# Loading and turning the first group's inputs in another way: attention with pooled keys into a mixture of four feed-forward branches

## The chip, the cores and the metric

The kernel runs on one core of one Trainium2 chip. The metric is the device time of one execution in microseconds; lower is better. Five engines work side by side, each on its own list of instructions: PE (matrix products, with weight loads shown as PEld), DVE (vector), ACT (scalar functions and copies), POOL and SP. Transfers between HBM and the on-chip memory are issued here by SP and by POOL and run on 16 DMA engines.

## The reference

```python
# attention: q, k, v are (8 batches, 8 heads, 576 tokens, 64)
k_p = k.reshape(B, H, 72, 8, D).mean(axis=3)      # 576 keys pooled to 72
v_p = v.reshape(B, H, 72, 8, D).mean(axis=3)
attn = softmax(q @ k_p.T / sqrt(64))              # over the 72 pooled keys
x = (attn @ v_p) -> rows (batch, token), columns (head, dim): 4608 x 512
# mixture: four branches, weighted by domain_probs
p = domain_probs / (domain_probs.sum(-1) + 1e-9)  # 4608 x 4
out = sum over e of p[:, e] * (relu(x @ w1[e]) @ w2[e])   # w1: 512 x 1024, w2: 1024 x 512
```

All inputs and the output are F32 in HBM; the products are done in bf16 with F32 sums.

## The kernel before

The 4608 tokens are cut into 36 tiles of 128, four tiles to a group of 512 tokens, nine groups. A step is one group with one branch, so there are 36 steps; each has 12 slots in which `up` (L457, eight blocks of `relu(x @ w1)`, ACT at L461) for the next step alternates with `down` (L490) and `collect` (L501, L505) of this step. Work of later tiles is put into slots by a hand-written plan (`at`, `plan_tile`, `plan_batch`). The order of every engine is the order in which the kernel writes its instructions; nothing reorders them.

Before the steps stands a head, also written out by hand, that gets group 0 through attention and through branch 0. For each tile t of group 0:

- the queries are cast to bf16 by ACT (`split_q`, L570) and turned by four PE products (`turn_q`, L310) and an ACT copy to `qT` (L314);
- `scores` (L320, one PSUM buffer `sc`), the maximum `maxima` (L334), the subtraction `less` (L338) on DVE, the exponential `expo` on ACT (L351 for tiles 0 and 1, L358 for 2 and 3);
- tiles 0 and 1: `attn_T` turns the unnormalised weights (L394, copy L395), `sums_by_products` gets the sums on PE (L640, L645, L647), `context_rows` multiplies by the values (L410) and divides (L419, `x_sb` in two halves), `turn_x` turns the result (L654) and ACT copies it into `xT` (L657);
- tiles 2 and 3: `normalise` divides on DVE first (L372 to L380), then `attn_T` and `context` (L440, copy to `xT` L446);
- `up_tile` (L473, relu L477) does the up-projection of one tile in two halves of four blocks, `down(0, t)` the second product, `collect(0, t)` the weighting.

The keys of batch 0 are folded from 8 to 1 on DVE in three parts of rows (`fold_keys0`, L589 and L593), turned on PE (`turn_keys0`, L600) and copied to `kT` by DVE (`take_keys0`, L613). The values are pooled by eight products with an identity (`sum_values0`, L619) and spread into a block form `vbd` by DVE (`spread_values0`, L628). `idle_products` (L576) are products with zeros that fill PE's waits.

The transfers of the head: SP loads all of group 0's queries in one transfer `qg` (L130), token `4p + c` on partition p, in pieces of 1 KB; then the domain weights of group 0 in the same token order (`dp0`, L134) and those of the other 32 tiles (`dpr`, L139). POOL loads, with conversion to bf16, the first keys (L80, L84: two parts and a tail), the first values, then builds the identity and the small mask `own`, then loads `w1[0]`, `w2[0]`, `w1[1]` and so on (L116, L122); from the ninth on each POOL load waits for the one eight before it.

The domain weights of group 0 are normalised by four small DVE operations in the head (`domain_probs0`, L205 to L208). Those of the other groups are normalised in slot 8 of step 0 on 32 partitions (`domain_probs`, L215 to L220), turned by four F32 products (L226) and copied (L227). Since group 0's tokens are permuted over its four tiles, `collect` writes its output rows with a stride of four rows.

Of the kernel before, what the change touches and what calls it, by code (L numbers as in the profile page):

```python
# [10 lines left out]
ALU = mybir.AluOpType  # L11
AX = mybir.AxisListType
BF16 = mybir.dt.bfloat16
F32 = mybir.dt.float32
# [3 lines left out]
def kernel(  # L18
# [70 lines left out]
    def load_v(b):  # L89
        load_rows(vraw[b % 2], v[b])  # L90
# [30 lines left out]
    def load_w2(e):  # L121
        nc.gpsimd.dma_start(  # L122
            out=w2_sb[e][:], in_=moe_w2[e].rearrange("(fb p) d -> p fb d", p=P)
        )

    qg = raw.tile([P, H, TPG, D], F32, name="qg")
    nc.sync.dma_start(  # L130
        out=qg[:], in_=q[0][:, 0:G, :].rearrange("h (p c) d -> p h c d", c=TPG)
    )
    dp0 = const.tile([P, TPG, E], F32, name="dp0")
    nc.sync.dma_start(  # L134
        out=dp0[:], in_=moe_domain_probs[0:G].rearrange("(p c) e -> p c e", c=TPG)
    )
    NL = NT - TPG
    dpr = const.tile([NL, P, E], F32, name="dpr")
    nc.sync.dma_start(  # L139
        out=dpr[:], in_=moe_domain_probs[G:NTOK].rearrange("(t p) e -> t p e", p=P)  # L140
    )

    still = const.tile([P, G], BF16, name="still")
    nc.vector.memset(still[:], 0.0)  # L144
    load_rows(kraw[0], k[0], ((0, 2), (2, 4)))
    load_v(0)
    ident = const.tile([P, P], BF16, name="ident")
    make_identity(nc, ident[:])

# [2 lines left out]
    for sign, base in ((1, 0), (-1, SP - 1)):  # L152
        nc.gpsimd.affine_select(
            out=own[:], in_=own[:], compare_op=ALU.is_ge, fill=0.0,
            base=base, channel_multiplier=sign,
            pattern=[[sign * (P - PW), NPAIR], [sign * P, 2], [-sign * SP, 2]],
        )
    load_w1(0)
    load_w2(0)
    load_w1(1)  # L160
    for c in range(TPG):
        qrow[c] = qpool.tile([P, H, D], BF16, name="qrow")
    load_k(1)
    ident32 = const.tile([NL, NL], F32, name="ident32")
    make_identity(nc, ident32[:])
    load_w1(2)
    load_q(TPG)
    load_w2(1)
# [31 lines left out]

    p_sb = const.tile([P, E, NT], F32, name="p_sb")

    def domain_probs0():
        ds0 = const.tile([P, TPG], F32, name="ds0")
        nc.vector.reduce_sum(out=ds0[:], in_=dp0[:], axis=AX.X)  # L205
        nc.vector.tensor_scalar_add(out=ds0[:], in0=ds0[:], scalar1=1e-9)
        nc.vector.reciprocal(out=ds0[:], in_=ds0[:])
        nc.vector.tensor_tensor(  # L208
            out=p_sb[:, :, 0:TPG].rearrange("p e c -> p c e"), in0=dp0[:],
            in1=ds0[:].unsqueeze(2).to_broadcast([P, TPG, E]), op=ALU.mult,  # L210
        )

    def domain_probs():
        dsum = const.tile([NL, P], F32, name="dsum")
        nc.vector.reduce_sum(out=dsum[:], in_=dpr[:], axis=AX.X)  # L215
        nc.vector.tensor_scalar_add(out=dsum[:], in0=dsum[:], scalar1=1e-9)
        dinv = const.tile([NL, P], F32, name="dinv")
        nc.vector.reciprocal(out=dinv[:], in_=dsum[:])
        pn = const.tile([NL, E, P], F32, name="pn")
        nc.vector.tensor_tensor(  # L220
            out=pn[:], in0=dpr[:].rearrange("t p e -> t e p"),
            in1=dinv[:].unsqueeze(1).to_broadcast([NL, E, P]), op=ALU.mult,
        )
        pt = ps_t.tile([P, E, NL], F32, tag="t", name="pt")
        for e in range(E):
            nc.tensor.transpose(pt[:, e, :], pn[:, e, :], ident32[:])  # L226
        nc.scalar.copy(out=p_sb[:, :, TPG:NT], in_=pt[:])  # L227


    kT, vbd, pads = {}, {}, {}  # L230
# [264 lines left out]
    def collect(s, i):  # L495
        g, e = divmod(s, E)
        t = g * TPG + i
        ps = o_ps[t]
        if e == 0:
            accs[t] = accp.tile([P, DM], F32, name="acc")  # L500
            nc.vector.tensor_scalar_mul(  # L501
                out=accs[t][:], in0=ps[:], scalar1=p_sb[:, e, t:t + 1]
            )
        else:
            nc.vector.scalar_tensor_tensor(  # L505
                out=accs[t][:], in0=ps[:], scalar=p_sb[:, e, t:t + 1], in1=accs[t][:],
                op0=ALU.mult, op1=ALU.add,
            )
        if e == E - 1:
            rows = out[t * P:(t + 1) * P, :]  # L510
            if g == 0:
                rows = out[0:G, :].rearrange("(p c) d -> p c d", c=TPG)[:, i, :]
            nc.sync.dma_start(out=rows, in_=accs[t][:])


    SLOTS = 12
# [2 lines left out]
    def at(slot, fn, *args):  # L519
        plan.setdefault(slot, []).append((fn, args))  # L520
# [21 lines left out]
            if t + 3 < NT:  # L542
                at(slot + sum_v, load_q, t + 3)

    at(SLOTS - 4, domain_probs)
    at(SLOTS - 2, prep_k, 1)
    at(SLOTS, prep_kT, 1)
    at(SLOTS + 4, prep_v, 1)
# [18 lines left out]


    def split_q(c):
        nc.scalar.copy(out=qrow[c][:], in_=qg[:, :, c, :])  # L570
# [13 lines left out]

    def fold_keys0(p1, i0, i1):
        rows = kraw[0][0:p1, i0:i1]
        for n in (4, 2):
            w = n * D
            nc.vector.tensor_add(  # L589
                out=rows[:, :, 0:w], in0=rows[:, :, 0:w], in1=rows[:, :, w:2 * w]  # L590
            )
        twice = [p1, i1 - i0, 2, D]
# [22 lines left out]

    def sum_values0():
        ps = ps_h.tile([P, NB, D], F32, tag="h", name="v_ps")
        for r in range(POOL):
            nc.tensor.matmul(  # L619
                ps[:], lhsT=ident[:], rhs=vraw[0][:, :, r * D:(r + 1) * D],  # L620
                start=(r == 0), stop=(r == POOL - 1),
            )
        return ps

    def spread_values0(ps):
        vbd[0] = prep.tile([P, NPAIR, 2, 2, D], BF16, name="vbd")
        for z in range(2):
            nc.vector.tensor_tensor(  # L628
                out=vbd[0][:, :, z],
                in0=ps[:, z:z + NPAIR].unsqueeze(2).to_broadcast([P, NPAIR, 2, D]),  # L630
                in1=mask_v[:, :, z], op=ALU.mult,
            )
# [15 lines left out]

    def turn_x(t, halves):
        n = KC // 2  # L650
        for i, pool, tag in ((0, ps_t, "t"), (1, ps_h, "h")):
            ps = pool.tile([P, n, P], BF16, tag=tag, name="xT_ps")
# [9 lines left out]
    idle_products(14)  # L662
    make_mask_v()
    split_q(0)
    split_q(1)
    turn_q(0)
    turn_q(1)
    for part in ((P, 0, 2), (P, 2, 4), (TAIL, 4, 5)):
        fold_keys0(*part)
        turn_keys0(*part)  # L670
        idle_products(2)
    take_keys0()
    scores(0)
    split_q(2)
    turn_q(2)
    idle_products(2)
    less_max(0)
    split_q(3)
    expo(0)
    spread_values0(sum_values0())  # L680
    scores(1)
    attn_T(0)
    maxima(1)
# [4 lines left out]
    turn_q(3)  # L688
    idle_products(1)
    turn_x(0, x_sb)  # L690
    less(1)
    expo(1)
    up_tile(0, 0, (0,))
    attn_T(1, copy=nc.vector.tensor_copy)
    up_tile(0, 0, (TPG,))
    sums_by_products(1)
    x_sb = context_rows(1, 2)
    scores(2)
    idle_products(2)
    turn_x(1, x_sb)  # L700
    less_max(2)
    expo(2)
    domain_probs0()
    up_tile(0, 1)
    scores(3)
    down(0, 0)
    normalise(2)
    less_max(3)
    collect(0, 0)
# [62 lines left out]
```

## Time and profile before

| | |
|---|---|
| median of 3 runs | 550.66 us (550.55 to 550.84) |
| profiled execution | 551.05 us |
| its span, first to last instruction | 548.6 us |
| granted TensorE clock, mean | 0.999 |
| busy PE, DVE, ACT, POOL | 536.1, 264.4, 213.0, 71.2 us |
| keys of batch 0 complete (end of the wait) | 9.38 us |
| first values product | 13.06 us |
| first `scores` | 12.15 us |
| first `up_tile` product | 18.43 us |
| first `up` product of step 1 | 35.57 us |

Times within the execution count from the first instruction. A line of the timeline gives the start, the length, the engine, the source line, what is written from what, the shapes, how many, and in brackets how long the engine had been idle and what ended that. A line of the chain gives the start, the length and the work that held the end of the program at that time.

### The profile page before, as it was taken

Reading aid. Unit: us, or ns where it says so; the run is one execution under the profiler, and the core shown is the slowest. Engines: PE = TensorE matmul, PEld = TensorE weight load, DVE = VectorE, ACT = ScalarE, POOL = GpSimd, SP = SyncE. Lnnn points to the kernel's source line nnn. Section 1 sums busy time; section 2 is a strip of 40 time slices with the busy share of each in tenths; the row PEclk is TensorE's granted clock in tenths of the full one; section 3 lists DMA queues with packets and bytes.
Section 4 is the critical chain, followed back from the end, with each engine's and each line's share of the span. In section 5 each row is a group of like instructions: output and inputs, shape, how many; then the busy total and the mean of one; then the engine's idle time right before and its main releaser. Section 6 shows DMA issues by size and latency. Waiting matters only on the chain.

```text
span 548.6 us, 7264 instructions
## 1 busy us (share of the span) xinstructions
PE 536.1 (98%) x2870; PEld 260.3 (47%) x2926; DVE 264.4 (48%) x458; ACT 213.0 (39%) x356; POOL 71.2 (13%) x120
## 2 busy tenths in 40 slices
PE   6899999999999999999999999999999999999997
PEld 2664554444444444444444444444444444444443
DVE  4775847444744446444554444744474444422223
ACT  3564653333333333333333333333333333333330
POOL 7234001121111101011011100101010000000000
PEclk9999999999999999999999999999999999999999
DMA  9999926656545553377436552335333421111002
GB/s 194 207 202 198 200 24 129 85 78 87 115 71 76 82 115 79 49 80 117 85 54 84 76 115 32 54 41 118 41 54 41 99 51 32 22 39 38 1 0 78
DMA packets 110689, 45.84 MB, mean 84 GB/s; under 512 B 87584, under 2 KB 106016, under 8 KB 110656
## 3 DMA queue, kind: packets, MB, share of 16 engines
q0 software_dynamic: 51472, 22.03, 32.8%
q1 hardware_dynamic: 59184, 23.35, 17.7%
q8 instruction: 23, 0.38, 0.3%
q14 instruction: 10, 0.08, 0.0%
HBM read 45.16 MB, written 9.44 MB: 100 GB/s over the span
## 4 chain that ended last, share of the span: by engine, by line
PE 95%; DMA 1%; DVE 1%; issue 1%; ACT 1%; POOL 0%; DVEq 0%; POOLq 0%
PE o_ps L490 45%; PE h_ps L457 44%; PE x_ps L410 2%; PE sc L320 2%; PE h_ps L473 1%; DMA kraw<-in_k_dram 1%; PE x_ps L440 1%; PE at_ps L394 0%; PE qT_ps L310 0%; ACT attnT L395 0%; ACT xT L657 0%; POOL kraw L80 0%; DVE mx L334 0%; DVE d_sb L338 0%; DVE acc L505 0%
## 5 line engine op out<-in xcount | busy, mean ns | idle before, releaser
L461 ACT ACTIVATE h_sb<-h_ps 128x512 bf16<-128x512 f32 x280 | 167.2, 597 | 296.5 <-PE h_ps L457 292.3
L457 PE MATMUL h_ps<-xT,w 128*128 128x512 bf16 x1088 | 271.8, 379 | 1.5
L490 PE MATMUL o_ps<-w,h_sb 128*128 128x512 bf16 x1130 | 270.0, 379 | 1.3
L490 PEld LDWEIGHTS <-h_sb 128*128 128x128 bf16 x1152 | 112.3, 98 | 133.8
L505 DVE SCALAR_TENSOR_TENSOR acc<-o_ps,p_sb,acc 128x512 f32<-128x512 f32 x108 | 81.0, 750 | 180.4 <-PE o_ps L490 177.7
L457 PEld LDWEIGHTS <-w 128*128 128x128 bf16 x1120 | 105.9, 98 | 116.9
L501 DVE TENSOR_SCALAR acc<-o_ps,p_sb 128x512 f32<-128x512 f32 x36 | 27.0, 749 | 59.6 <-PE o_ps L490 59.6
L529 POOL COPY gated<-x_sb0of 1x1 bf16<-1x1 bf16 x28 | 7.8, 279 | 365.5 <-DVE x_sb0of L419 365.5
L108 POOL DMA_DIRECT2D qrow<-in_q_dram x36 | 30.6, 852 | 26.0 <-DMA w<-in_moe_w_dram 10.5
L334 DVE TENSOR_REDUCE mx<-sc 128x8 f32<-128x576 f32 x36 | 27.2, 756 | 11.1 <-PE sc L320 11.1
L338 DVE TENSOR_TENSOR d_sb<-sc,mx 128x576 f32<-128x576 f32 x36 | 27.3, 757 | 1.3
L419 DVE SCALAR_TENSOR_TENSOR x_sb0of<-x_ps,rs 128x512 bf16<-128x512 f32 (+1 forms) x30 | 20.2, 674 | 12.4 <-PE x_ps L410 11.7
L351 ACT ACTIVATE attn<-d_sb 128x576 bf16<-128x576 f32 x30 | 20.5, 683 | 3.5 <-DVE d_sb L338 0.3
L372 DVE TENSOR_REDUCE es<-attn 128x8 f32<-128x576 bf16 x28 | 20.8, 743 | 0.0
L410 PEld LDWEIGHTS <-attnT 128*128 128x128 bf16 (+1 forms) x165 | 12.4, 100 | 7.2 <-issue 1.3
L320 PE MATMUL sc<-kT,qT 128*128 128x144 bf16 (+1 forms) x160 | 15.0, 227 | 0.2 <-DVE kT L613 0.2
L410 PE MATMUL x_ps<-vbd,attnT 128*128 128x192 bf16 (+5 forms) x165 | 15.2, 231 | 0.0
L320 PEld LDWEIGHTS <-qT 128*128 128x128 bf16 (+1 forms) x160 | 11.1, 100 | 8.6 <-issue 2.2
L576 PE MATMUL o_ps<-still 128*128 128x512 bf16 x27 | 9.3, 458 | 1.3 <-DVE still L144 1.3
L235 DVE TENSOR_TENSOR vraw<-vraw 128x1280 bf16<-128x1280 bf16 (+1 forms) x14 | 9.2, 654 | 0.2
L235 DVE TENSOR_TENSOR kraw<-kraw 128x1280 bf16<-128x1280 bf16 (+1 forms) x14 | 8.9, 639 | 0.2
L473 PE MATMUL h_ps<-xT,w 128*128 128x128 bf16 x128 | 8.3, 219 | 0.2
(80 smaller groups left out, 147.5 us busy)
## 6 DMA issues: line engine op xcount, KB each, us to landing
out_dram<-acc SPq DMA_DIRECT2D x36, 256.0 KB, 2.1
vraw<-in_v_dram POOLq DMA_DIRECT2D x8, 512.0 KB, 7.4
w<-in_moe_w_dram POOLq DMA_DIRECT2D x8, 512.0 KB, 15.9
w<-in_moe_w_dram POOLq DMA_DIRECT2D x4, 1024.0 KB, 16.1
kraw<-in_k_dram POOLq DMA_DIRECT2D x7, 512.0 KB, 8.0
qrow<-in_q_dram POOLq DMA_DIRECT2D x28, 128.0 KB, 4.0
qg<-in_q_dram SPq DMA_DIRECT2D x1, 1024.0 KB, 6.1
kraw<-in_k_dram POOLq DMA_DIRECT2D x2, 256.0 KB, 7.0
```

The lines of the kernel that those rows point to most:

```text
L108: nc.gpsimd.dma_start(out=qrow[t][at:at + n], in_=q[b][:, tok:tok + n, :].rearrange("h p d -> p h d"),)
L320: nc.tensor.matmul(sc[at:at + n, pair // 2, (pair % 2) * PW:(pair % 2 + 1) * PW], lhsT=qT[t][:, pair, at:at + n], rhs=kT[b][:].rearrange(" ...
L334: nc.vector.reduce_max(out=mxs[t][:], in_=by_head(t), axis=AX.X)
L338: nc.vector.tensor_tensor(out=st[t][:], in0=by_head(t), in1=mxs[t][:].unsqueeze(3).to_broadcast([P, 2, 4, SP]), op=ALU.subtract,)
L351: nc.scalar.activation(out=attn[t % 2][:, 0:ROWS].rearrange("p (h j) -> p h j", j=SP), in_=st[t][:].rearrange("p g h j -> p (g h) j"), fun ...
L372: nc.vector.reduce_sum(out=es[:], in_=e, axis=AX.X)
L410: nc.tensor.matmul(ps[at:at + n, h0 * D:(h0 + c1 - c0) * D], lhsT=attnT[t][:, i, at:at + n], rhs=flat[:, c0 * D:c1 * D], start=(i == 0), s ...
L457: nc.tensor.matmul(ps[:], lhsT=w1_sb[e][:, kc, fb * P:(fb + 1) * P], rhs=xT[g][:, kc, :], start=(kc == 0), stop=(kc == KC - 1),)
L461: nc.scalar.activation(out=hs[s][:, fb, :], in_=ps[:], func=ACT.Relu)
L490: nc.tensor.matmul(ps[:], lhsT=hs[s][:, fb, i * P:(i + 1) * P], rhs=w2_sb[e][:, fb, :], start=(fb == 0), stop=(fb == FB - 1),)
L501: nc.vector.tensor_scalar_mul(out=accs[t][:], in0=ps[:], scalar1=p_sb[:, e, t:t + 1])
L505: nc.vector.scalar_tensor_tensor(out=accs[t][:], in0=ps[:], scalar=p_sb[:, e, t:t + 1], in1=accs[t][:], op0=ALU.mult, op1=ALU.add,)
```

## The change

Six things change, all of them in the head or taken into it.

1. Group 0's tokens keep their order. Each tile's queries come in a transfer of its own as pieces of 8 consecutive tokens of one head (2 KB): `qf[c]`, 128 rows (head, block of 8 tokens). Tiles 0 and 1 are loaded by SP, tiles 2 and 3 by POOL between its loads of values and weights.
2. A tile of queries is turned by 16 products: for each of the 8 tokens r of a block and each of two head parities z, the 64 columns `qrow[c][:, r]` are the weights and 64 chosen columns of the identity are what streams; the results go to partitions 0 to 63 or 64 to 127. `take_q0` copies the result to `qT` in token order.
3. The first keys are loaded in F32 by SP behind the first tile of queries (tail first, then two pairs of blocks); the first fold on DVE reads F32 and writes bf16, the rest stays.
4. POOL builds the identity and `own` first and loads the values in three parts behind them; the values are summed in two passes, over blocks 0 and 1 and then over 2 to 4. `w2[0]` is loaded in two halves.
5. All 36 tiles of domain weights are loaded first on SP, turned raw in the head by four F32 products (the F32 identity is a DVE copy of a corner of the bf16 one), copied by ACT and normalised on 128 partitions by four DVE operations; nothing of them is left in step 0.
6. The order of the head changes with it: tile 3's queries are turned between the halves of `up_tile(0, 1)`, `scores(3)` stands behind `down(0, 0)`, `turn_x` uses two buffers of one PSUM pool, idle products are set anew.

```diff
-    nc.sync.dma_start(
-        out=qg[:], in_=q[0][:, 0:G, :].rearrange("h (p c) d -> p h c d", c=TPG)
-    )
...
+    R = POOL
+    NC = P // R
+    qf = [raw.tile([P, R, D], F32, name=f"qf{c}") for c in range(TPG)]
+    def load_q0(c, queue):
+        queue.dma_start(
+            out=qf[c][:].rearrange("p r d -> p (r d)"),
+            in_=q[0][:, c * P:(c + 1) * P, :].rearrange("h (c r) d -> h c (r d)", r=R),
+        )
+    dpr = const.tile([NT, P, E], F32, name="dpr")
+    nc.sync.dma_start(out=dpr[:], in_=moe_domain_probs.rearrange("(t p) e -> t p e", p=P))
+    load_q0(0, nc.sync)
+    kf = raw.tile([P, NB, POOL * D], F32, name="kf")
+    rows0 = k[0].rearrange("h (j r) d -> (h j) (r d)", r=POOL)
+    nc.sync.dma_start(out=kf[0:TAIL, NB - 1, :], in_=rows0[(NB - 1) * P:ROWS])
+    for i in (0, 2):
+        nc.sync.dma_start(
+            out=kf[:, i:i + 2, :],
+            in_=rows0[i * P:(i + 2) * P].rearrange("(i p) x -> p i x", p=P),
+        )
+    load_q0(1, nc.sync)
-    load_rows(kraw[0], k[0], ((0, 2), (2, 4)))
-    load_v(0)
     ident = const.tile([P, P], BF16, name="ident")
     make_identity(nc, ident[:])
...
+    load_rows(vraw[0], v[0], ((0, 2), (2, 4)))
+    load_q0(2, nc.gpsimd)
     load_w1(0)
-    load_w2(0)
+    load_q0(3, nc.gpsimd)
+    load_w2(0, 2)
     load_w1(1)
...
+    def turn_probs():
+        ident32 = const.tile([NT, NT], F32, name="ident32")
+        nc.vector.tensor_copy(out=ident32[:], in_=ident[0:NT, 0:NT])
+        ps = ps_s.tile([P, E, NT], F32, tag="sc", name="pt")
+        for e in range(E):
+            nc.tensor.transpose(ps[:, e, :], dpr[:, :, e], ident32[:])
+        pt = const.tile([P, E, NT], F32, name="pt_sb")
+        nc.scalar.copy(out=pt[:], in_=ps[:])
+        return pt
...
-    at(SLOTS - 4, domain_probs)
...
+    def turn_q0(c):
+        ps = ps_t.tile([P, R, NPAIR, NC], F32, tag="t", name="qT_ps")
+        heads = ident[:].rearrange("x (a z c) -> x a z c", z=2, c=NC)
+        for r in range(R):
+            for z in range(2):
+                nc.tensor.matmul(
+                    ps[z * D:(z + 1) * D, r], lhsT=qrow[c][:, r], rhs=heads[:, :, z],
+                    start=True, stop=True,
+                )
+        return ps
...
-    for part in ((P, 0, 2), (P, 2, 4), (TAIL, 4, 5)):
+    for part in ((TAIL, 4, 5), (P, 0, 2), (P, 2, 4)):
         fold_keys0(*part)
...
-    domain_probs0()
-    up_tile(0, 1)
+    up_tile(0, 1, (0,))
+    take_q0(3, turn_q0(3))
+    up_tile(0, 1, (TPG,))
+    down(0, 0)
     scores(3)
-    down(0, 0)
     normalise(2)
```

More of the change, by code (lines that the diff above doesn't have):

```diff
@@ L119, in load_w1, with load_w2 @@
             )
-    def load_w2(e):
-        nc.gpsimd.dma_start(
-            out=w2_sb[e][:], in_=moe_w2[e].rearrange("(fb p) d -> p fb d", p=P)
-        )
-    qg = raw.tile([P, H, TPG, D], F32, name="qg")
-    nc.sync.dma_start(
-        out=qg[:], in_=q[0][:, 0:G, :].rearrange("h (p c) d -> p h c d", c=TPG)
-    )
[L133 to L141, printed above, removed]
+    def load_w2(e, parts=1):
+        n = FB // parts
+        for f0 in range(0, FB, n):
+            nc.gpsimd.dma_start(
+                out=w2_sb[e][:, f0:f0 + n],
+                in_=moe_w2[e].rearrange("(fb p) d -> p fb d", p=P)[:, f0:f0 + n],
+            )
[6 more added lines that the diff above has]
+            in_=q[0][:, c * P:(c + 1) * P, :].rearrange("h (c r) d -> h c (r d)", r=R),
+        )
+    dpr = const.tile([NT, P, E], F32, name="dpr")
[10 more added lines that the diff above has]
+    load_q0(1, nc.sync)
     still = const.tile([P, G], BF16, name="still")
     nc.vector.memset(still[:], 0.0)
-    load_rows(kraw[0], k[0], ((0, 2), (2, 4)))
-    load_v(0)
     ident = const.tile([P, P], BF16, name="ident")
@@ L157 @@
         )
+    load_rows(vraw[0], v[0], ((0, 2), (2, 4)))
+    load_q0(2, nc.gpsimd)
     load_w1(0)
-    load_w2(0)
+    load_q0(3, nc.gpsimd)
+    load_w2(0, 2)
     load_w1(1)
     for c in range(TPG):
-        qrow[c] = qpool.tile([P, H, D], BF16, name="qrow")
+        qrow[c] = qpool.tile([P, R, D], BF16, name="qrow")
     load_k(1)
-    ident32 = const.tile([NL, NL], F32, name="ident32")
-    make_identity(nc, ident32[:])
     load_w1(2)
@@ L201, with domain_probs @@
     p_sb = const.tile([P, E, NT], F32, name="p_sb")
[L203 to L207, printed above, removed]
+    def turn_probs():
[7 more added lines that the diff above has]
+        return pt
+    def domain_probs(pt):
+        by_tile = pt[:].rearrange("p e t -> p t e")
+        dsum = const.tile([P, NT], F32, name="dsum")
+        nc.vector.reduce_sum(out=dsum[:], in_=by_tile, axis=AX.X)
+        nc.vector.tensor_scalar_add(out=dsum[:], in0=dsum[:], scalar1=1e-9)
+        nc.vector.reciprocal(out=dsum[:], in_=dsum[:])
         nc.vector.tensor_tensor(
-            out=p_sb[:, :, 0:TPG].rearrange("p e c -> p c e"), in0=dp0[:],
-            in1=ds0[:].unsqueeze(2).to_broadcast([P, TPG, E]), op=ALU.mult,
-        )
[L213 to L227, printed above, removed]
+            out=p_sb[:], in0=pt[:], in1=dsum[:].unsqueeze(1).to_broadcast([P, E, NT]),
+            op=ALU.mult,
+        )
     kT, vbd, pads = {}, {}, {}
@@ L509, in collect @@
         if e == E - 1:
[L510 to L513, printed above, removed]
+            nc.sync.dma_start(out=out[t * P:(t + 1) * P, :], in_=accs[t][:])
     SLOTS = 12
@@ L569, in split_q, with take_q0 @@
     def split_q(c):
-        nc.scalar.copy(out=qrow[c][:], in_=qg[:, :, c, :])
+        nc.scalar.copy(out=qrow[c][:], in_=qf[c][:])
+    def turn_q0(c):
[8 more added lines that the diff above has]
+        return ps
+    def take_q0(c, ps):
+        qT[c] = qtp.tile([P, NPAIR, P], BF16, name="qT")
+        nc.scalar.copy(
+            out=qT[c][:].rearrange("x a (c r) -> x a c r", r=R),
+            in_=ps[:].rearrange("x r a c -> x a c r"),
+        )
     def idle_products(n):
@@ L586, in fold_keys0 @@
         rows = kraw[0][0:p1, i0:i1]
+        src = kf[0:p1, i0:i1]
         for n in (4, 2):
@@ L589, in fold_keys0 @@
             nc.vector.tensor_add(
-                out=rows[:, :, 0:w], in0=rows[:, :, 0:w], in1=rows[:, :, w:2 * w]
+                out=rows[:, :, 0:w], in0=src[:, :, 0:w], in1=src[:, :, w:2 * w]
             )
+            src = rows
         twice = [p1, i1 - i0, 2, D]
@@ L617, in sum_values0 @@
         ps = ps_h.tile([P, NB, D], F32, tag="h", name="v_ps")
[L618 to L622, printed above, removed]
+        for part in (slice(0, 2), slice(2, NB)):
+            for r in range(POOL):
+                nc.tensor.matmul(
+                    ps[:, part], lhsT=ident[:], rhs=vraw[0][:, part, r * D:(r + 1) * D],
+                    start=(r == 0), stop=(r == POOL - 1),
+                )
         return ps
@@ L650, in turn_x @@
         n = KC // 2
-        for i, pool, tag in ((0, ps_t, "t"), (1, ps_h, "h")):
-            ps = pool.tile([P, n, P], BF16, tag=tag, name="xT_ps")
+        for i in range(2):
+            ps = ps_h.tile([P, n, P], BF16, tag="h", name="xT_ps")
             for kc in range(n):
@@ L660, in turn_x @@
         idle_products(1)
-    idle_products(14)
+    idle_products(10)
+    pt = turn_probs()
     make_mask_v()
     split_q(0)
-    split_q(1)
-    turn_q(0)
-    turn_q(1)
-    for part in ((P, 0, 2), (P, 2, 4), (TAIL, 4, 5)):
+    idle_products(2)
+    take_q0(0, turn_q0(0))
+    for part in ((TAIL, 4, 5), (P, 0, 2), (P, 2, 4)):
         fold_keys0(*part)
@@ L673 @@
     scores(0)
-    split_q(2)
-    turn_q(2)
-    idle_products(2)
+    split_q(1)
+    take_q0(1, turn_q0(1))
     less_max(0)
-    split_q(3)
     expo(0)
+    idle_products(1)
     spread_values0(sum_values0())
@@ L682 @@
     attn_T(0)
+    split_q(2)
     maxima(1)
@@ L687 @@
     x_sb = context_rows(0, 2)
-    turn_q(3)
+    qT_ps = turn_q0(2)
     idle_products(1)
@@ L692 @@
     expo(1)
+    take_q0(2, qT_ps)
+    domain_probs(pt)
     up_tile(0, 0, (0,))
@@ L695 @@
     up_tile(0, 0, (TPG,))
+    split_q(3)
     sums_by_products(1)
@@ L698 @@
     scores(2)
-    idle_products(2)
+    idle_products(1)
     turn_x(1, x_sb)
```

## The prediction
> **What bounds the kernel now.** I read the page's totals and chain first, to see which engine carries the span and from when.
>
> ```profile
> span 548.6 us, 7264 instructions
> PE 536.1 (98%) x2870; PEld 260.3 (47%) x2926; DVE 264.4 (48%) x458; ACT 213.0 (39%) x356; POOL 71.2 (13%) x120
> PE 95%; DMA 1%; DVE 1%; issue 1%; ACT 1%; POOL 0%; DVEq 0%; POOLq 0%
> ```
>
> PE carries 95% of the chain. What is not PE must lie in the first microseconds, so I read the chain in order of time there (start, length, what):
>
> ```profile
> 2.16 7.23 DMA kraw<-in_k_dram
> ...
> 12.15 0.42 PE sc L320 x4
> ...
> 14.92 0.47 PE at_ps L394 x5
> ...
> 18.43 0.27 PE h_ps L473 x2
> 18.70 0.00 issue
> 18.70 0.94 PE h_ps L473 x14
> ...
> 29.42 1.80 PE h_ps L473 x32
> ...
> 40.91 0.36 PE pt L226 x4
> ...
> 48.79 0.38 PE sc L320 x8
> ```
>
> The keys' transfer holds everything to 9.38; then tile 0's softmax and turns alternate between engines until the first up-projection at 18.43. From `up_tile(0, 1)` at 23.02 PE hardly stops. So the change is worth what the head up to there gains, less PE work added behind it, plus PE work removed (the four `pt` products at 40.91). The timeline shows that the keys were not alone:
>
> ```profile
> 13.01 0.96 PEld L619 LDWEIGHTS <-ident 128*128 128x128 bf16 x8 [0.28 <-DMA vraw<-in_v_dram]
> 14.19 0.68 ACT L351 ACTIVATE attn<-d_sb 128x576 bf16<-128x576 f32 x1 [0.26 <-DVE d_sb L338]
> 14.34 1.29 DVE L628 TENSOR_TENSOR vbd<-v_ps,mask_v 128x512 bf16<-128x512 f32 x2 [0.19 <-PE v_ps L619]
> 17.00 0.42 DVE L419 SCALAR_TENSOR_TENSOR x_sb0of<-x_ps,rs 128x256 bf16<-128x256 f32 x1
> ```
>
> The values land at 13.0 and PE waits for them too; value products and `scores(1)` end at 14.63, 0.3 before the keys' path opens `at_ps`. Bringing only the keys forward buys 0.3. The windows (PE, PEld, DVE, ACT, POOL, clock, DMA share, GB/s) give the rates:
>
> ```profile
> 4.00:5.00 1.00, 1.00 (x5) 0.32 (x3) 0.00 (x0) 0.00 (x0) 0.96 (x3) 1.00 1.08 378
> 9.00:10.00 1.00, 0.72 (x4) 0.23 (x4) 0.76 (x3) 0.66 (x2) 0.78 (x2) 1.00 1.20 195
> ```
>
> In the first only SP's F32 queries move (378 GB/s); in the second only POOL's converting loads (195 to 210 written as bf16, so about 400 read). DMA is full from 3 to 40 us: arrivals go by bytes queued ahead.
>
> **Keys.** SP's queue becomes domain weights 0.07 MB, query tile 0 0.26, key tail 0.13, keys 2 x 0.52, query tile 1 0.26: 1.52 MB to the last key. The page's first 0.4 us slices with traffic moved 10, 84, 120 and 223 GB/s, 0.175 MB by 3.2; the other 1.34 MB at 378 take 3.5: 6.8. POOL's first load was issued at 1.33, its first packets came after 5.0; now `ident` and `own` (4.70 to 6.03, 1.33 us) go ahead of the values, so their bytes come from about 6.3 and share the end. I take 7.3, between 6.8 and 9.4 (no gain). The first fold reads F32: 0.69 by L338's 0.757 for 576 F32 elements, against 0.43 (0.43 to 0.76). Fold 0.69 + 0.30, `kpad` 0.29, turn 0.28, two copies 0.62, `scores(0)` 0.42, maximum and subtraction 1.54, exponential 0.69 and hand-overs end near 12.5, against 14.88.
>
> **Values.** Up to their end 1.78 MB from SP and 1.18 are ahead, 2.96 MB, where there were 3.49 (1.05 queries, 0.08 weights, 2 x 1.18). 0.53 MB less at 400 GB/s is 1.3 us: 11.65. By another sum, SP has moved 1.35 MB by 6.3, 1.61 MB follow at 400: 10.3, plus the 1.6 by which the same sum falls short of 13.0 for before: 11.9. The upper end is 13.4, as late as before and the POOL work not absorbed. I take 12.2. The second eight value products have 192 columns: 0.66 and 0.17 to the result, 13.06 (all eight of before, 1.25). `vbd` 1.24, maximum of tile 1 0.75, sums 0.17 + 0.20 with hand-overs 0.5, `x_sb` 0.36 + 0.34: 16.3. Turn and copy of the second half: 17.0; first up group done 17.95, against 19.64. **The head gains 1.67**, or 2.2 with values at 11.65, 0.5 at 13.4.
>
> The Trainium skill (DMA: Bandwidth & Descriptors, section "Why a DMA increments its semaphore by 16 and not by 1") speaks against this: a copy runs on the largest number of engines up to 16 that divides the slowest dimension of both sides. The query tiles' source has eight heads outermost, so by it they run on 8 engines, which then (an estimate from that page) carry 218 KB each up to the last value, as all 16 did before; values near 13.0 would make the sum 550.7. No row of before shows it.
>
> **Turning the queries.** Sixteen products with 64-column weights a tile take the place of four. Nearest row: `scores` of the tile that spans two batches, 64-column weights, 8 in 0.38, 48 ns: 0.76 a tile. Bounds: 29 ns (the 16 `x_ps` products of 64 columns at 58.89, 0.47) and 58.5 ns (16 in 0.94): 0.47 to 0.94. Tile 0's is hidden by the wait for keys, tile 1's by the wait for values, tile 2's by DVE making `x_sb`: `x_ps` ends near 14.65, 0.76 and one idle product 0.22 make 15.65, before 15.97. Without that cover each would cost its 0.76. Tile 3's stands between the halves of `up_tile(0, 1)` and is paid. ACT's splits and takes (0.6 each) replace four casts and four copies of equal length; split 3 falls between `h_sb` and `xT`, where ACT idled 0.82.
>
> **Order behind it.** `scores(3)` moves behind `down(0, 0)`. Before, 23.02 to 29.42 was PE's own work, 6.40. After: up 0.93, turn 0.76, up 0.93, down 1.73, scores 0.25 + 0.17 = 4.77; then `up_tile(0, 2)` needs `xT` of tile 2, which ACT copies after the exponential of tile 3: 0.75 + 0.76 + 0.69 + 0.59 with hand-overs 2.95, where PE has only 2.6 of work. 7.72, **a loss of 1.32** (1.03 to 1.50 by the turn's bounds). Had DVE been late anyway, part would be nothing; but `normalise(2)` is through by then.
>
> **Domain weights.** The `pt` products leave step 1: **gain 0.36**. In the head they stand among idle products, covered by the wait for queries; uncovered 0.4. On DVE 2.9 us at 34.65 to 37.59 go, off the path (`kT` of batch 1 is used at 45.5). Four operations, about 1.15, come between `less(1)` and the copy of `attnT(1)`, and end 0.2 before that copy can start; uncovered at most 0.5.
>
> **Weights.** POOL's waits show `w1[0]` complete near 18.3 and `w2[0]` at 23.4. Ahead of the first 0.27 MB less: 17.6, needed 18.2; the second, same bytes, needed for its second half at 24.8. Output rows of group 0 keep their 2 KB pieces: nothing.
>
> **Sum.** 1.67 - 1.32 + 0.36 = 0.7 less. The profiled execution took 551.05, 2.45 of it outside the span, and stands 0.39 above the median 550.66; 550.35 for it is 550.0 on the median's scale. A change under 0.2% (1.1 us) is about what cannot be told from none.
>
> **Rivals.** *Values ride with the bytes* (0.25): they land at 11.65 or sooner with turns at 29 to 48 ns; the gain of 0.7 grows to 1.2 to 2.2, 548.5 to 549.5. For: bytes ahead are all that set arrivals in before. Against: POOL starts its stream later. *Queries clog the stream* (0.15): values near 13.0, `w1[0]` after 18.9, head gain 0.9 or less, 550.5 to 551.5; for it, four more transfers among loads that already fill DMA; against, no row shows an uneven queue. *SP's issues come too slowly* (0.2), the slower side: SP rows show 0.46 for the queries' issue but 1.2 for its transposes. With 1.2 each for the first query tile, tail and first key pair, the last pair is issued near 4.9 and lands with `qg`'s 6.1 at 11.0; the exponential ends at 16.2, `at_ps` 1.3 later than before, and with 1.32 paid and 0.36 saved it ends at 552.9. It binds once the last key lands after about 8.3 and outweighs the rest from about 9.0. For it: three of the issues are new shapes. Against: every plain SP load of the head took 0.42 to 0.56.
>
> ```profile
> 0.82 0.46 SPq L130 DMA_DIRECT2D qg<-in_q_dram  x1
> ...
> 83.44 1.26 SPq L304 DMA_TRANSPOSE qT<-qrow  x1
> ```
>
> **How the numbers follow.** My case (0.4) spans 549.4 to 550.4; a quarter of it is faster by over 0.2%. Faster: 0.25 + 0.1 = 0.35. Slower: 0.2 and a little of the clogged case, 0.22. Same: 0.43. The range takes the first rival nearly whole and the milder half of the slow one: 548.5 to 552.3.
>
> **What would show it.** Right: the last key near 7.3, the value products' second wait ending near 12.2, first up group done near 18, `scores(3)` followed by a PE wait of about 0.4 before `up_tile(0, 2)`, no `pt` after 40. Wrong: a value or `w1` wait of PE longer than before's 0.28, SP issues over 1 us, idle products still 0.43 apart (as before 5.0, against 0.215 later) after 7 us, or turns of 16 over 0.94.

## The result and the profile after

The changed kernel takes 558.51 us (558.05 to 558.99, 4 runs) against 550.75 us (550.55 to 550.84, 4 runs) for the kernel before: ratio 1.0139, interval 1.0127 to 1.0151, 7.8 us slower. 550.0 was predicted, between 548.5 and 552.3. The profiled execution took 558.5, 7.45 more than that of before (551.05), in a span of 556.5 where there were 548.6.

The page's totals first (span; busy time by engine; shares of the chain that ended last):

```profile
span 556.5 us, 7425 instructions
PE 542.1 (97%) x2978; PEld 262.5 (47%) x2978; DVE 262.7 (47%) x455; ACT 212.9 (38%) x356; POOL 71.0 (13%) x119
PE 94%; DMA 3%; ACT 1%; DVE 1%; SPq 0%; issue 0%; DVEq 0%
```

DMA's share of the chain has gone from 1% to 3%. The chain in order of time (start, length, what) says which transfer it is, 14.11 us where the longest of before was 7.23:

```profile
3.78 14.11 DMA qf<-in_q_dram
17.91 0.63 ACT qrow L571
...
19.76 2.09 PE v_ps L642 x16
...
25.82 0.94 PE h_ps L478 x14
...
37.26 1.96 PE h_ps L478 x32
```

The transfer that holds everything is not that of the keys but the queries of **tile 1**, issued by SP at 3.78, last in its queue, and complete at 17.89. Four instructions from the timeline show who waits behind it (in brackets the idle time before, and what ended it):

```profile
13.05 0.69 DVE L610 TENSOR_TENSOR kraw<-kf 128x512 bf16<-128x512 f32 x1 [2.35 <-DMA kf<-in_k_dram]
15.55 0.64 PE L325 MATMUL sc<-kT,qT 128*128 128x144 bf16 x4
17.91 0.62 ACT L571 CAST qrow<-qf 128x512 bf16<-128x512 f32 x1 [9.83 <-DMA qf<-in_q_dram]
19.75 0.69 ACT L356 ACTIVATE attn<-d_sb 128x576 bf16<-128x576 f32 x1
```

The last key lands at 13.05 (9.38 before), the first `scores` start at 15.55 (12.15). Tile 0's subtraction is done at 17.78, but ACT's list has the cast and the copy of tile 1's queries ahead of tile 0's exponential, and PE's has their turn ahead of the value products. So both tiles stand behind one late transfer, and the value products (their transfers had landed at 13.5) start at 19.56 instead of 13.06. From there the loss is carried along: first `up_tile` after tile 0's turn of `xT` 25.82 (18.70 for the same group before), `up_tile(0, 2)` 37.26 (29.42), last `collect` 552.47 (544.94), 7.53 later.

The windows (PE, PEld, DVE, ACT, POOL, clock, DMA share, GB/s) show the transfers and the second change. In the changed kernel:

```profile
3.00:4.00 1.00, 1.00 (x4) 0.40 (x3) 0.00 (x0) 0.00 (x0) 1.00 (x2) 1.00 0.40 111
4.00:5.00 1.00, 1.00 (x5) 0.25 (x2) 0.00 (x0) 0.00 (x0) 1.00 (x3) 1.00 0.99 229
9.00:10.00 1.00, 0.02 (x1) 0.00 (x0) 0.64 (x1) 0.00 (x0) 0.58 (x1) 0.50 1.14 283
```

In the kernel before, from 3 to 4:

```profile
3.00:4.00 1.00, 1.00 (x4) 0.41 (x3) 0.00 (x0) 0.00 (x0) 1.00 (x2) 1.00 0.99 327
```

From 4 to 5 us, 229 GB/s moved where there were 378; from 3 to 4 it was 111 where there were 327. And the granted clock is 0.50 from 8 to about 21.6 us; before, the windows show 1.00 throughout. (In both kernels the idle products up to about 4.7 us were 0.43 apart, and later ones 0.21, under the same 1.00: the windows do not show that first stretch.) The sixteen value products took 2.09 in the chain. Last, how the two queues stood to each other from 9 to 10 us (packets, MB, share of the time of 16 engines; q0 is POOL's queue, q1 is SP's):

```profile
q0 software_dynamic: 92, 0.09, 57.8%
q1 hardware_dynamic: 92, 0.19, 55.9%
```

Packet for packet the same. In the kernel before, POOL's queue had this window to itself, and the keys shared it with nothing:

```profile
q0 software_dynamic: 192, 0.19, 120.0%
```

### The profile page after: what moved, and what is told of

Its sections match the earlier page's. It is cut to its first block, busy times and chain, and to the rows that moved or that the text cites. A ratio compares the mean times of both kernels' runs of the same rounds, so it can differ in the third digit from the quotient of the medians.

```text
span 556.5 us, 7425 instructions
## 1 busy us (share of the span) xinstructions
PE 542.1 (97%) x2978; PEld 262.5 (47%) x2978; DVE 262.7 (47%) x455; ACT 212.9 (38%) x356; POOL 71.0 (13%) x119
## 3 DMA queue, kind: packets, MB, share of 16 engines
q1 hardware_dynamic: 58896, 24.01, 17.6%
## 4 chain that ended last, share of the span: by engine, by line
PE 94%; DMA 3%; ACT 1%; DVE 1%; SPq 0%; issue 0%; DVEq 0%
PE o_ps L495 44%; PE h_ps L462 44%; DMA qf<-in_q_dram 3%; PE x_ps L415 2%; PE sc L325 2%; PE h_ps L478 1%; PE x_ps L445 0%; PE v_ps L642 0%; DVE mx L339 0%; ACT xT L680 0%; PE at_ps L399 0%; DVE vbd L651 0%; ACT h_sb L482 0%; ACT qrow L571 0%; PE qT_ps L315 0%; SPq L148 0%
## 5 line engine op out<-in xcount | busy, mean ns | idle before, releaser
L339 DVE TENSOR_REDUCE mx<-sc 128x8 f32<-128x576 f32 x36 | 27.2, 756 | 12.2 <-PE sc L325 12.2
L424 DVE SCALAR_TENSOR_TENSOR x_sb0of<-x_ps,rs 128x512 bf16<-128x512 f32 (+1 forms) x30 | 20.2, 674 | 12.4 <-PE x_ps L415 11.7
```

The source lines that it names most:

```text
L339: nc.vector.reduce_max(out=mxs[t][:], in_=by_head(t), axis=AX.X)
```

## The experiments

Each kernel starts from one of the two, and its diff, shortened here, shows what differs; one measures transfers alone. The instants of the main ones beside each other, each from one profiled execution; the last column is the median of all runs:

| kernel | keys: last wait ends | tile 1's queries | first `scores` | first value product | us |
|---|---|---|---|---|---|
| before | 9.38 | one transfer, 6.93 | 12.15 | 13.06 | 550.75 |
| changed | 13.05 | 17.89 | 15.55 | 19.56 | 558.51 |
| before, with only the keys on SP | 13.86 | one transfer, 6.44 | 16.40 | 18.11 | 556.74 |
| changed, keys back on POOL | 10.6 | 10.9 | 13.92 | 15.51 | 553.71 |
| the same, query tiles on 16 engines | landed by 8.3 | by 9.4 | 12.00 | 12.94 | 551.09 |
| before, with only the weights | 9.02 | one transfer, 6.38 | 11.86 | 12.76 | 549.87 |

### One part at a time: the keys

Keys in F32 on SP, alone, in the kernel before:

```
     dpr, qg, dp0 on SP as before
+    kf: tail, blocks 0-1, blocks 2-3 in F32 on SP
-    load_rows(kraw[0], ...); load_v(0) ahead of ident
+    load_v(0) behind ident and own
```

> The kernel before with one part of the change: the first keys in F32 on SP (tail first, then two pairs of blocks) behind the one query transfer and the weights; POOL begins with the identity, then the values. Theory 1 (two queues share the engines by halves): SP has 2.3 MB up to the last key, of which some 0.4 MB moves before POOL's first packets at 4.0 to 4.5 and the rest at about half of 400 GB/s until POOL's values (1.18 MB) and then its weights take turns: last key at 12 to 14, `scores(0)` about 3 to 4 later than before's 12.15, 553 to 556. Theory 2 (query tiles alone): SP's bytes go first as the prediction had it, 2.3 MB at 378 GB/s from 2.4, last key near 8.8, and the time is that of before or a little less, 550 to 551.

Measured: 556.74 us, ratio 1.011 (1.0097 to 1.0123). The chain, and the queues from 9 to 10 us:

```profile
3.62 10.24 DMA kf<-in_k_dram
```
```profile
q0 software_dynamic: 86, 0.09, 57.3%
q1 hardware_dynamic: 87, 0.17, 50.9%
```

Up to 5 us SP has the engines alone and moves 0.36 to 0.38 MB a microsecond, as the prediction assumed. From 6 to 7 POOL's queue takes most of the engines and SP moves 0.04; then, up to 12, 0.17 to 0.21, because every second packet is POOL's. The last key lands at 13.86, inside the 12 to 14 of theory 1 and 5 us from theory 2. This part alone costs 6.1 us; the total is 0.7 above theory 1's range, and the clock, 0.50 from 11.3 to 18.1, was not in it.

### The keys given back

The changed kernel with the keys, and the values behind them, back on POOL ahead of the identity, and the folds reading bf16:

```
-    kf: three F32 loads on SP
+    load_rows(kraw[0], k[0], ((0, 2), (2, 4)))
+    load_rows(vraw[0], v[0], ((0, 2), (2, 4)))
     ident, own
```

> The changed kernel with the first keys given back to POOL (converting, ahead of the values, both ahead of the identity as before); query tiles, turns, weights and order of the head as changed. SP then has only the weights and two query tiles, 0.6 MB. Theory 1 (the keys' 1.18 MB stood behind 0.33 MB on SP's queue, which got half the engines or less once POOL's loads began at 4.0 us): the keys lead POOL's queue and nothing of POOL is ahead of them, so they land at 9 to 10, values near 13, PE keeps its clock, and what remains of the loss is the query turn and the order behind it, 0.7, less 0.5 for the `pt` products: 550.5 to 552. Theory 2 (the 2 KB query tiles on half of the engines are the cause): tile 1's queries still end after 10 and keys after 10.5, and most of the loss stays: 554 to 558.

Measured: 553.71 us, ratio 1.0052 (1.0038 to 1.0067). 4.8 of the 7.8 us are gone, but neither theory's range holds it alone: keys at 10.6, tile 1 at 10.9. The queues from 4 to 5 us:

```profile
q0 software_dynamic: 129, 0.12, 75.4%
q1 hardware_dynamic: 41, 0.08, 25.7%
```

SP has only 0.6 MB to move and moves it at 0.08 to 0.10 MB a microsecond from 4 to 9 us, with a quarter of the engines' time (24 to 30%); POOL's queue, whose first packets came after 5 us before, is running by 3 to 4, and gets 0.07 to 0.15 instead of 0.20. That opened two questions, one run each.

**The shape of a query tile.** Only the order of the transfer's dimensions changes, and the identity's columns are copied once (0.27 on DVE) so that the turn streams them contiguously:

```
-            in_=q[0][...].rearrange("h (c r) d -> h c (r d)", r=R),
+            in_=q[0][...].rearrange("h (c r) d -> c h (r d)", r=R),
+    nc.vector.tensor_copy(out=heads[:], in_=ident[:].rearrange("x (c a z) -> x z a c", ...))
```

> The kernel with the keys back on POOL (553.7), with the query tiles loaded with their 16 blocks of tokens outermost instead of the 8 heads, and the identity columns that turn them copied once by DVE into the order in which they stream (so the turn stays at some 0.4). Theory 1 (a tile with 8 outermost moves on 8 engines, slowly, beside POOL's loads, which start at 3 to 4 us because the other half is free): SP's 0.6 MB now moves at over 0.3 MB a microsecond from 3 us and ends near 5 to 6, POOL's first packets come when it ends, the last key lands at 9.4 or sooner and PE keeps its clock but for a short gap: 550.5 to 551.5. Theory 2 (SP's queue takes turns with POOL's whatever its shape): tile 1's queries still land after 8, keys after 10, half clock from 10: 553 to 554.

Measured: 551.09 us, ratio 1.0009 (1.0000 to 1.0019): 2.6 less by the shape of four small transfers, inside theory 1's range. The queues from 3 to 4 us:

```profile
q1 hardware_dynamic: 102, 0.20, 86.6%
q0 software_dynamic: 7, 0.01, 4.3%
```

SP moves 0.20 MB where the 8-outermost shape moved 0.04 in that microsecond, with POOL held to 7 packets. Then the two take turns in bursts, and SP is done by 7 us, not 5 to 6, at 0.24 MB a microsecond at most, not over 0.3; after that POOL's queue is alone, at 0.20 as before. No fold of the keys waits any more (the second starts at 8.34). `scores` still start only at 12.00, because PE had fallen to 0.50 from 8.1 to about 11.5 and two pairs of idle products, 0.85 a pair in the chain, stand ahead of the last turn of keys.

**The clock.** Idle products added so that PE does not rest:

```
-    idle_products(2) ahead of turn_q0(0); 2, 2, 2 behind the three parts of the keys
+    idle_products(4); 9, 3, 2; and 2 ahead of scores(0)
```

> The kernel with the keys back on POOL (553.7) with more idle products (4 ahead of the first turn, 9, 3 and 2 behind the three parts of the keys, 2 ahead of the scores), no load changed. If the fall to half clock (0.50 from 9.6 to 17 us: idle products of 0.43 twice two on the path, scores 0.69 instead of 0.41, value products 1.80 instead of 1.1) takes 1 to 1.5 of the loss: clock 1.00 throughout, keys still at 10.6, 552.2 to 552.8. If waits for transfers hide it: 553.5 to 553.9.

Measured: 552.91 us (552.09 to 553.70), ratio 1.0046 (1.0029 to 1.0062). In the profiled execution the clock was 1.00 throughout and the keys landed at 10.17. The gain over 553.71 is 0.8 in the median, a little less than expected; the spread of the runs leaves its size loose. And that it is the clock's is not shown: of the four executions with the keys back, three had a mean clock of 0.994 and took 553.25 to 553.87, and the fourth, at 1.000, took 553.87. With the tiles on 16 engines, too, the two of ten executions at 1.000 took 550.99 and 551.57, the others, at 0.995 to 0.997, 550.94 to 551.17.

### One part at a time: the weights

The kernel before, with the 32 other tiles' domain weights turned raw in the head and normalised on 128 partitions there:

```
-    at(SLOTS - 4, domain_probs)
+    pt = turn_probs()          # behind turn_q(1), 4 F32 products
...
     domain_probs0()
+    domain_probs(pt)
```

> The kernel before with one part of the change: the domain weights of the other 32 tiles are turned raw in the head (after the second query turn) and normalised on 128 partitions; nothing of them is left in step 0. From the prediction's term: 0.36 to 0.55 less than the kernel before, 550.1 to 550.3. Rival (the head has no room, or it was hidden anyway): no difference or up to 0.4 more.

Measured: 549.87 us, ratio 0.9984 (0.9974 to 0.9993) over 12 runs: 0.86 less, and the one version here that beats both kernels. Step 1 begins 0.3 earlier than before (35.43 for 35.73 in the chain), and the `pt` products and what stood around them, about 0.5, are gone from it. That half is the expected one. The other 0.3 goes with keys that landed at 9.02 instead of 9.38; why they did, with no load of theirs changed, is not shown.

### Inside the changed kernel

**The queries of tiles 0 and 1 issued by ACT** instead of SP (`load_q0(0, nc.scalar)`, `load_q0(1, nc.scalar)`):

> The changed kernel with the queries of tiles 0 and 1 issued by ACT instead of SP, shape unchanged; the keys are then alone on SP behind the domain weights. Theory (a slow query transfer holds what is queued behind it on its own queue): the keys land at 5 to 7.5, the tile-1 queries still 4 to 8 us after tile 0's, at 10 to 14; time 552 to 556. Rival (the slow transfer occupies the shared engines whatever queue it is on): the last key stays after 11; time 557 or more.

555.72 us (one execution). Tile 1's queries come at 11.66, 6.2 earlier, the keys at 12.18, only 0.9 earlier, against the theory. So not SP's issuing and not tile 1's place in the queue alone: with it mended, the keys are the next to be late.

**Idle products against the half clock** (12, 14 and 2 behind the three parts of the keys, and 8 between `scores(0)` and tile 1's turn):

> The changed kernel with more idle products in the three long waits of PE (12, 14 and 8 in the places of 2, 2 and 0), transfers untouched. Theory (late queries are the cause, the half clock an addition): the clock stays at 1.00, the queries of tile 1 still land near 17.9, the value products take 1.1 instead of 2.1, time 556.5 to 557.5. Rival (the half clock is most of the loss): 553 or less.

555.86 us (one execution), clock 0.999, value products 1.12. The keys are at 12.80; tile 1's queries came at 16.4 in this execution, 1.5 earlier, so perhaps less than half of the 2.65 gained is the clock's.

**POOL's loads held back.** A POOL copy that reads the last key part stands ahead of what is behind the values, or ahead of the values:

```
+    first = const.tile([1, 1], F32, name="first")
+    nc.gpsimd.tensor_copy(out=first[:], in_=kf[0:1, 3, 0:1])
```

> The changed kernel, but POOL waits for the last key part before it issues anything behind the values (queries of tiles 2 and 3, w1, w2). Theory (SP's queue and POOL's share the engines piece by piece, so POOL's bytes delay the keys though they are issued later): with 1.18 MB instead of 4 MB on POOL's queue the last key lands near 10 instead of 13.0, the values near 10 to 11, tile 1's queries near 12 instead of 17.9; time 552 to 555. Rival (SP's own queue is slow, whatever POOL does): last key at 12.5 or later, time 557 or more.

555.94 us (one execution) with the values still beside: keys at 12.07, tile 1 at 13.22, only 1.0 and 4.7 earlier, and between the two ranges. The values' 1.18 MB alone are enough to share.

> The same wait one step earlier: POOL issues no load at all, the values included, before the last key has landed. Theory (sharing): SP alone moves its 1.5 MB, the last key lands at 7 to 8, tile 1's queries at 9 to 10; values about 5 us after the last key, 12.5 to 13.5; time 552 to 556, bounded by weights. Rival (SP's own queue is slow): last key still after 11.

555.49 us (one execution) with nothing of POOL beside. Alone on the engines, SP's list brings the last key at 9.61, not at 7.3. In the chain the wait is then for `w1[0]`, from 13.82 to 23.80. In 2 to 4 us its windows show a DMA share of only 0.41 and 0.19 MB moved, and from 8.5 to 9.5, where by the bytes little more than tile 1's queries is left, 102 packets with 52.8% of the engines' time.

**The blocks outermost**, in the changed kernel (keys still on SP, identity columns read with a stride):

> The changed kernel with the four query transfers written with the 16 blocks of tokens outermost instead of the 8 heads; same bytes, same pieces, same order of the queues. Theory (shape): tile 0's queries land near 3.7 instead of 6.3, the last key near 7.5 instead of 13.0, tile 1's queries near 9 instead of 17.9, values about 12; granted clock 1.00 throughout; time 549 to 551. Rival (bytes ahead on SP, or SP's queue against POOL's): the last key still after 11 and tile 1's queries after 14; time 556 or more. Rival (the clock is the cause and the transfers only its occasion): the clock still falls to 0.50 after 8 us; time above 555.

558.3 us, ratio 1.014 (1.0123 to 1.0157): a miss. Tile 1's queries came at 15.73, 2.2 earlier, but the keys later, at 14.23, and each turn of 16 took 1.03 to 1.1 where it takes 0.37 to 0.44 with contiguous columns; three such turns stand in the chain, so part of what the shape may have freed went there. With the keys on SP the shape of the tiles did not bring the keys forward: the two halves of the change each keep the head late without the other.

**Blocks outermost, POOL held behind the values, and idle products (4, 8, 2, 3)** together:

> The changed kernel with blocks of tokens outermost in the query transfers, POOL's wait for the last key behind the values, and idle products 4, 8, 2 and 3 in the waits. Theory (shape and sharing together make the loss, the clock the rest): last key near 9.5, tile 1's queries near 10.5, clock 1.00, time 549.5 to 552. Rival (something else in the changed head costs): 554 or more.

556.28 us, ratio 1.01 (1.0081 to 1.0119): a miss. Keys at 12.83, and PE was at 0.50 from 10.7 to 17.6 in the profiled execution, so that eight idle products took 3.41 in the chain: set to keep the clock, they became the delay. But that execution was the slowest of the four (557.93, mean clock 0.994); the other three kept 0.999 and took 555.73 to 556.45. So most of the miss is not the clock's. Three turns of 1.03 stand in the chain here too; how the rest divides is not shown.

### A transfer by itself

Only transfers, one at a time, each waiting for the one before; attention and mixture are left out. Each moves 256 KB to 128 partitions in pieces of 2 KB; the dimension that stands outermost in the source differs:

> Only transfers, one after the other, each issued when the one before has landed: 256 KB in 128 pieces of 2 KB on SP with plain rows (plain128), with 16 blocks of tokens outermost (blocks16x8), with 8, 4 and 2 heads outermost, then 64 and 36 plain rows, then two on POOL; twice round. The attention and the mixture are left out. Theory (the heads-outermost shape is itself slow): plain128 and blocks16x8 land 2.0 to 3.0 us after issue, heads8x16 4 to 5 us, heads4x32 and heads2x64 longer still, 6 to 11 us; the same on POOL. Rival (the shape costs nothing, only the other traffic of the head delays it): all five within 0.5 us of one another.

```profile
3.62 3.55 DMA blocks16x8r<-in_q_dram
...
7.45 4.14 DMA heads8x16r<-in_q_dram
```

These are the chain's lines for 16 and 8 outermost. With 16, 8, 4 and 2: 3.55, 4.14, 5.56, 7.52 (second pass 3.48, 4.28, 5.30, 7.87). Each halving adds 0.6 to 0.8, 1.0 to 1.4 and 2.0 to 2.6, about twice the step before, as when 8, 16 and 32 more pieces wait in line at each engine that is left. So the Trainium skill's rule (DMA: Bandwidth & Descriptors, section "Why a DMA increments its semaphore by 16 and not by 1") holds here. The share of the 16 engines' time says the same: 0.67 with 16 outermost (5 to 6 us), 0.43 with 8 (9 to 10), 0.25 with 4 (15 to 16) and 0.13 with 2 (22 to 23). Plain rows, expected to be like 16 blocks, were faster, 2.44 and 2.68. But alone, a tile on 8 engines costs only 0.6 to 0.8 us more; the 2.6 us appear beside another queue.

### What could be kept of the change

The weights, the tail of the keys first (on POOL) and the values in three loads and two passes, in the kernel before:

```
+    load_rows(kraw[0], k[0], ((0, 2), (2, 4)), True)     # tail first
+    load_rows(vraw[0], v[0], ((0, 2), (2, 4)))
-    for part in ((P, 0, 2), (P, 2, 4), (TAIL, 4, 5)):
+    for part in ((TAIL, 4, 5), (P, 0, 2), (P, 2, 4)):
```

> The kernel before with the parts of the change that move no load to SP: domain weights turned in the head (as in the run with the weights alone), the tail of the first keys loaded and folded first, the first values loaded in three parts and summed in two passes. Loads keep their queue and their bytes. If keys land as in the run with the weights alone (all by 9.0), the last fold of 64 rows (0.75 on DVE) no longer stands between the last part and `scores(0)`: first `scores` 0.5 to 0.7 earlier than its 11.86, `at_ps` at 14.0 instead of 14.62, values (landed near 12.3) take 0.85 instead of 1.25: 549.1 to 549.6. If the values' arrival or DVE's order binds instead: 549.8 to 550.0.

A miss: 553.1 us, ratio 1.0042 (1.0024 to 1.0059), and the 12 runs spread from 550.09 to 555.85. In the profiled execution (554.42) the wait for blocks 2 and 3 of the keys ends at 9.85 instead of 9.02: the tail's load now goes ahead of them and costs what its fold saves, and the head ends 0.26 later than with the weights alone (35.69 for 35.43 at the first product of step 1). The rest is not in the head at all:

```profile
311.73 0.14 PEld L463 LDWEIGHTS <-w 128*128 128x128 bf16 x2 [3.29 <-issue]
```

From the end of a product at 308.94, PE stands still for 2.8 us in the middle of the steps, and runs at 0.50 until 314.4. The timeline names nothing that it waits for ("issue"), but the landing times do. The products at 311.76 read the next group's `xT`, whose last quarter SP turns by a transfer issued at 303.71. It landed 8.0 us later, at 311.71, where the median of the 28 such transfers is 2.5. From 306 to 313 the transfers and queues were:

```profile
q0 software_dynamic: 1645, 0.72, 98.9%
q1 hardware_dynamic: 56, 0.01, 1.0%
vraw<-in_v_dram POOLq DMA_DIRECT2D x1, 512.0 KB, 6.3
xT<-x_sb0of SPq DMA_TRANSPOSE x1, 8.0
```

So this is once more a small transfer of SP beside a stream of POOL, here a later load of values. In the run with the weights alone the same two stand beside each other and the transfer lands after 2.5; SP's issue of it took 1.19 there and 2.45 here. Why it fell behind in this execution stays open.

## Why the prediction was wrong

By its own steps, with what the runs showed:

- **Keys at 7.3: the step that failed.** The sum let SP's 1.52 MB go at 378 GB/s as bytes queued ahead of POOL's. Three things were wrong in it. Two queues do not stand one behind the other, they share: 92 packets against 92. POOL's packets begin at 4.0 to 4.5, not at 6.3 (at 3.0 to 3.5 with the keys back, where its first load is issued at 1.33 instead of 2.04). And SP's rate with the small tiles in front is 111 GB/s at 3 to 4 us, not 327. Alone the list ends at 9.61, with the values beside it at 12.07, with all of POOL's loads at 13.05: of the 5.75 us between 7.3 and 13.05, 2.3 are the list's own slowness and 3.4 the sharing. The upper bound, 9.4 for no gain, was taken from before, where nothing shared with the keys; it was no bound for a transfer that changes queues. The same sum with half the rate from 4.5 us on gives 9.0, and the slow start (0.20 MB moved by 4.0, where the sum had 0.48) another 1.5 at 0.19 MB a microsecond; how the last 2.5 divide was not measured.
- **The Trainium skill** has this rule too (DMA: Bandwidth & Descriptors, section "Queues, rings and completion order"): each engine takes turns between the queues that have work for it, a packet at a time. The windows agree, once both streams run; the prediction did not use it.
- **Tile 1's turn hidden by the wait for values: failed by the same step.** Its transfer was counted with the others at 378 GB/s, and no time of its own was worked out for it; it landed at 17.89 and held ACT's and PE's lists. The change put a wait in two in-order lists, and what stood behind it, tile 0's exponential and the value products, was not priced.
- **Values at 12.2:** they landed at 13.5, within 0.1 of the bound of 13.4, but by luck: the bound was for POOL's work not absorbed, and they were late because they shared the engines. They were not what bound, and "values ride with the bytes" falls with them.
- **The head's gain of 1.67** became a loss of 7.12 (first up group done 26.76 for 19.64). (From its own figures, 19.64 less 17.95, the gain is 1.69.) Undone one after the other: keys back on POOL 4.8, the tiles on 16 engines 2.6. What is left is 0.6 by the medians (0 to 1.0 by the interval of 551.09), and 0.11 between the two profiled executions at the first `down` of step 1 (43.22 for 43.11): the head 0.30 earlier than before, the order behind it 0.72 and the way to step 1 0.16 later, the `pt` products 0.47 less.
- **The clock** was taken as 1.00, and appears only among the signs of being wrong. Idle products alone brought 0.8 with the keys back and at most 2.65, of which 1.5 may be the earlier queries, in the changed kernel; and an execution with the keys back that kept 1.000 was no faster than the three that did not. The fall is a consequence: with idle products in PE's waits the clock stayed at 1.00. What it costs is not shown.
- **Sixteen turns at 0.76 a tile:** 0.37 at full clock (23 ns a product), below the lower bound of 0.47. **The order behind it** lost 0.72 (30.14 to 37.26 is 7.12, before 6.40), not 1.32; the mechanism held, with PE waiting 0.24 for `xT` of tile 2, and 0.39 of the difference is the turn.
- **The `pt` products, 0.36:** right, about 0.5 in the trace, 0.86 with the start of step 1 in the run of that part alone.
- **Weights and DVE:** `w1[0]` came at 22.18, long before the 25.5 that the head had become; covered, though later than 17.6. The four operations on DVE end at 26.96, and the copy of `attnT(1)` starts at 27.07: covered, as forecast.
- **The other rivals:** SP's issues took 0.43 to 0.73, so that rival falls. "Queries clog the stream" saw the uneven tiles, but put them at 550.5 to 551.5, as load on 8 engines in one ordered stream; their shape alone measured 2.6 us, since the other queue takes the free half and then shares the rest.

Sum in the measured terms: 7.12 + 0.72 + 0.16 (up to step 1) - 0.48 (the `pt` products' place) = 7.52, against 7.53 at the last `collect`.

Open: why POOL's queue gets nothing until 5 us while SP's stream fills all 16 engines, and then takes 82 to 93% of their time from 5 to 6.5 us in the changed kernel; the runs show the pattern, not the reason. And why the keys came later with the blocks outermost (14.23 for 13.05).

## What to carry to other kernels

Moving a transfer to a second queue does not put it ahead: it gives up its place in an ordered queue for a half share against everything that the first queue now starts beside it. Before splitting a load into tiles, look at which of its dimensions stands outermost, and price each new wait by what is behind it in its engine's list. And test a many-part change part by part: here one part of six was worth 0.86 us, and was buried under two, the keys on SP (6.1 alone in the kernel before) and the shape of the query tiles (2.6 once the keys were back).

## What was not expected of the hardware

- A transfer on half of the engines lost more beside another queue than alone: 0.08 to 0.10 MB a microsecond for five microseconds, against 256 KB in 4.1 to 4.4 us by itself with its latency.
- A turn whose streamed columns lie 8 apart took 64 to 69 ns a product, with contiguous ones 23, at full clock.
- The granted clock fell to 0.50 at 8.0 us in the changed kernel, after rests of PE of only 0.66 and 0.40, and stayed at 1.00 in the kernel before through one of 1.37 (up to 7.60). Once down, by the clock in windows of 1 us, it stayed down for about 3.4 us (8.1 to 11.5 with the tiles on 16 engines), 6.8 (9.8 to 16.6 with the keys back), 10.2 (10.0 to 20.2 with the blocks outermost) or 13.7 (8.0 to 21.6 in the changed kernel): multiples of the shortest. Groups of two idle products in between did not bring it back.
